# One core, mLSTM cell and squared-relu network: three moves in the main loop's transfer order, one in its vector order

## The chip, the cores and the metric

The kernel runs on one core of a Trainium2 chip. The metric is the device time of one execution in microseconds (us); lower is better. The kernel before has 11 timed runs with a median of 527.36 us (521.49 to 529.7), and one further execution was profiled.

## What is computed

The reference chains two blocks. The first is a gated recurrence (an mLSTM cell) over 4 batches, 8 heads, 768 positions and a head size of 40; the second is a network with a squared relu on the 3072 rows (batch times position) of 320 (head times size) that come out of it.

```python
C = f_stab * C + i_stab * outer(vt, kt);  n = f_stab * n + i_stab * kt
y[:, :, t] = sigmoid(o_gate[:, :, t]) * (C @ qt) / maximum(abs(n . qt), 1)
...
x = y.transpose(0, 2, 1, 3).reshape(3072, 320)
h = maximum(x @ w_in, 0)            # w_in 320 x 2048
out = (h * h) @ w_out               # w_out 2048 x 320
```

## The kernel before, in words

**Tiles and groups.** The rows are cut into 24 tiles of 128 positions, six to a batch. A tile's recurrence is computed in chunk form: scores of k and q (L424), weighted by decays (P_sb, L437), products with v and with the carried state C (L523, L534), and a new state (L512, L551; a batch's first tile copies it, L553, and has no L523; its last has no L512). Two tiles make a group of the network, 12 groups in all. The first network layer of a group is made in four steps (`ffn1_main` L649, `ffn1_rest` L660); the second layer (L743) uses seven half-size products instead of eight, in four steps of `ffn2_fast`, with the additions L759 and L738 on VectorE.

**Order.** The schedule is written out by hand: each engine runs its instructions in the order of the program. The main loop (L1002) takes group g in eight turns r = 0 to 7: r = 0 and 1 are steps 0 and 1 of group g's second layer, r = 2 to 5 the first layer of group g + 2 with the recurrence of two tiles in it, r = 6 and 7 steps 2 and 3. With b = 9, 11, ... for g = 1, 2, ..., the recurrence in g is that of tiles b and b + 1. The last groups have no first layer, and g = 11 is the last.

**Round trips.** Nearly all transfers of the main loop are issued by SP, one after the other, and an issue that has to wait holds up all behind it. Four kinds of data go through DRAM to be rearranged in 32 x 32 squares, and VectorE then turns the squares in place:

- x of a tile: `store_rows` (L613, one DMA), then `load_rows` (L618, four DMAs, which wait until the store has landed), then `turn_squares` (L625, xT), without which `ffn1_main` (L649) of that group can't start;
- the numerators of a tile: `store_num` (L557, one DMA), `load_num` (L562, four DMAs, into kq), then `normalise_turned` (L574 to L583), which makes x_sb;
- k and q of a tile: `pair_up` (L287, four DMAs from DRAM to DRAM, kq_rows: these are the squares' stores), `load_squares` (L309, four DMAs, kqT), then `turn_kq` (L316);
- the result: y_sb, of which the pool holds three and each group takes two. Its first half is stored in step 2 (L779, y1), its second in step 3 (L784, y0). The y0 of a group lies in the buffer of the y1 of the group before, so that step 0's addition (L759 with y_sb<-h_ps,y_sb) waits until that y1 has landed.

In the program a DMA of SP also waits for the eighth DMA before it.

**Order around the change.** In turn r = 0 of a group from g = 2 on, `normalise_turned` and `store_rows` of tile b - 1 are called behind step 0, and in r = 1 the turn of x of tile b - 2 ahead of step 1 (L1044), or for g = 2 behind it (L1119). The first layer in r = 2 is that of tiles b - 3 and b - 2. The squares of r = 1's `pair_up` are loaded in r = 2 (L1130) and turned in r = 4 (L1048), behind which VectorE has four squarings (L682), a turn of x, the normalising of tile b in r = 5 (L1050), the weighting of the scores of tile b + 2 and step 2's additions. The lines that are changed are these:

```python
        elif r == 1 and g > 2:                # L1044, ahead of the step
            do(turn_squares, b - 2)
...
        elif r == 1:                          # L1117, behind the step
            if g > 1:
                if g == 2:
                    turn_squares(9)
                do(load_rows, b - 1)
                do(pair_up, b + 2)
...
        elif r == 5:                          # L1147
            do(store_num, b + 1)
            if b > 9:
                do(load_rows, b)
                do(load_num, b + 1)
```

Of the kernel before, what the change touches and what calls it, by code (L numbers as in the profile page):

```python
# [29 lines left out]
def kernel(  # L30
# [283 lines left out]
    def turn_kq(s):  # L314
        t = kqT_b[s % NKT][:].rearrange("p n j t -> p (n j t)")
        nc.vector.transpose(t, t)  # L316
# [39 lines left out]
    def mask(s):  # L356

        A = st[s]["A"][0]
        nc.gpsimd.affine_select(  # L359
            A[:], A[:], compare_op=ALU.is_ge, fill=-1e30, base=0, pattern=[[0, H], [1, P]], channel_multiplier=-1,  # L360
        )

    def decays(s):

        if s % NB > 0:
            e = st[s]["eA"] = kq_b[2 + s % 2][:, 1].rearrange("p (j two) d -> p j (two d)", two=2)
            for i in range(2):
                rows = slice(DP * i, DP * (i + 1))
                nc.scalar.activation(e[rows], st[s]["A"][0][rows, PR * i : PR * (i + 1), :], AF.Exp)  # L369
# [112 lines left out]
    def scale_q(s):  # L482
        if s % NB > 0:
            d = st[s]
            nc.vector.tensor_tensor(d["eA"], d["eA"], d["qT"], op=ALU.mult)

    def decay_C(s):
        if s % NB > 0:
            Cd = st[s]["Cd"] = attn.tile([P, PR, D1], F32, name="Cd", bufs=1)
            nc.gpsimd.tensor_tensor(  # L490
                Cd[:], C_b[(s - 1) % 2][:, : PR * D1].rearrange("p (j d) -> p j d", d=D1),
                st[s]["eA"][:, :, P - 1 : P].to_broadcast([P, PR, D1]), op=ALU.mult,
            )
# [117 lines left out]
    def store_rows(s):  # L611
        t = st[s]["xT"] = xT_half(s).rearrange("p c t -> p (c t)")
        nc.sync.dma_start(x_d[s].rearrange("c t d -> t c d"), st[s]["x"][:].rearrange("p (c d) -> p c d", c=3))  # L613
# [9 lines left out]
    def turn_squares(s):  # L623
        t = st[s]["xT"]
        nc.vector.transpose(t, t)  # L625
        del st[s]
# [51 lines left out]
    def square_half():  # L678
        if st.get("relu"):
            rs, g4 = st["relu"].pop(0)  # L680
            for i, r in enumerate(rs):
                nc.vector.tensor_tensor(g4[:, :, i, :], r[:], r[:], op=ALU.mult)  # L682
# [104 lines left out]
    def do(f, s):  # L787
        if 0 <= s < NT:
            f(s)

    def score(s):
        scores(s)
        weighted(s)
# [185 lines left out]
    def attended(s, early=False):  # L979
        do(store_num, s)  # L980
        do(load, s + 4)
        do(load_num, s)
        if early:
            load_squares(s + 2)
            load_A(s + 2)
        do(pair_up, s + 3)
# [11 lines left out]
    def masked_W(s):  # L998
        weigh(s, masked=True)

    ALL = slice(0, NPAIR)
    for n, (which, g, i) in enumerate(parts):  # L1002
        s, at = 6 + n // 4, n % 4

        r, b = (n % 8, 7 + 2 * (n // 8)) if n >= 8 else (None, None)
        if n == 5:
            brought.close()
            late = ctx.enter_context(tc.tile_pool(name="late", bufs=1, side="right"))
        if n in (0, 4, 8):
            score(s)  # L1010
            if n == 4:
                square_half()
                square_half()
        if n in (2, 5):
            attend_turned(s)
            decays(s + 1)
            mask(s + 1)
            if n > 4:
                turn_kq(s + 1)
            decay_C(s + 1)  # L1020
            if s > X_SQ:
                turn_squares(s - 1)
            attended(s, early=(n == 5))
        if n == 6:
            scale_q(s + 1)
        if 5 <= n < 8:
            sums_of_weights(n - 5)
        if n == 6:
            sums(1, ALL, (1, 2))
        if n == 8:  # L1030
            load_squares(10)
            load_A(10)
            sums_of_weights(3)
            sums(1, ALL, (3,))
        if n == 9:
            score(9)
            attend_turned(8)
            decay_C(9)
            attended(8)
            turn_squares(7)  # L1040

        if r == 0 and g > 1:
            sums(g, ALL, (3,))
        elif r == 1 and g > 2:  # L1044
            do(turn_squares, b - 2)
        elif r == 4:
            do(scale_q, b + 1)
            do(turn_kq, b + 2)  # L1048
        elif r == 5 and b > 9:
            do(normalise_turned, b)  # L1050
            do(store_rows, b)
        elif r == 7 and g < NG - 1:
            sums(g + 1, ALL, (2,))
        if g == NG - 2 and which == 2 and i == 3:
            sums(g + 1, ALL, (2,))
        if which == 2 and g == NG - 1 and i == 0:
            sums(g, ALL, (3,))

        if which == 1:
            ffn1_main(g, i)  # L1060
            if i % 2 == 0:
                st["held"] = st["half"]
            elif r is None:
                ffn1_batch(g, i)
                if n != 3:
                    square_half()
                    square_half()
            else:
                x = b + i // 2

                def tiled():
                    do(score, x + 1)
                    do(attend_turned, x)

                ffn1_batch(g, i, tiled)
                do(decay_C, x + 1)
        elif g == 0:
            ffn2(g, *divmod(i, 2))
        else:
            ffn2_fast(g, i)  # L1080

        if n in (2, 6):
            masked_W(s + 1)
            if n < 4:
                turn_kq(s + 1)
                scale_q(s + 1)
            normalise_turned(s)
            store_rows(s)
            if n == 2:
                load_squares(s + 2)  # L1090
            load_rows(s)
            if n == 2:
                load_A(s + 2)
        if n == 7:
            for t in range(8, 12):
                sigmoid(t)
            decays(9)
            mask(9)
            turn_kq(9)
        if n == 8:  # L1100
            masked_W(9)
        elif n == 9:
            load_A(11)
            load_o(12)
            load_o(13)
            decays(10)
            mask(10)
        elif n == 10:
            normalise_turned(8)
            store_rows(8)  # L1110
        if r == 0 and g > 1:
            do(decays, b + 1)
            do(mask, b + 1)
            square_half()
            do(normalise_turned, b - 1)
            do(store_rows, b - 1)
        elif r == 1:  # L1117
            if g > 1:
                if g == 2:  # L1119
                    turn_squares(9)  # L1120
                do(load_rows, b - 1)
                do(pair_up, b + 2)
            square_half()
            if g < NG:
                sums(g, ALL, (4,))
            do(scale_q, b)
            do(turn_kq, b + 1)
        elif r == 2:
            do(masked_W, b + 1)
            do(load_squares, b + 2)  # L1130
            if n == 10:
                load_rows(8)
        elif r == 3:
            do(decays, b + 2)
            do(mask, b + 2)
            attended(b)
            if b % 4 == 3:
                for t in range(b + 1, min(b + 5, NT)):
                    sigmoid(t)
        elif r == 4:  # L1140
            square_half()
            square_half()
            do(masked_W, b + 2)
            do(load_A, b + 3)
            if b > 9:
                do(turn_squares, b - 1)
        elif r == 5:  # L1147
            do(store_num, b + 1)
            if b > 9:
                do(load_rows, b)  # L1150
                do(load_num, b + 1)
        elif r == 6 and b == 9:
            normalise_turned(9)
            store_rows(9)
            load_num(10)
            load_rows(9)
            load(14)
            turn_squares(8)
        elif r == 7 and b == 9:
            load_o(14)  # L1160
            load_o(15)
            load_squares(12)
            load_A(13)
        elif r == 6:
            do(load, b + 5)
            for t in range(b + 5, min(b + 7, NT)):
                load_o(t)
            do(load_squares, b + 3)
        elif r == 7:
            do(load_A, b + 4)  # L1170
        if which == 2 and g == NG - 1 and i == 0:
            sums(g, ALL, (4,))
        if n < 5:
            while rounding.done < LAST[n]:
                rounding.step(ahead=rounding.done + 1 < LAST[2])
# [30 lines left out]
```

## Time and profile before

| | |
|---|---|
| median of 11 runs (lowest, highest) | 527.36 us (521.49, 529.7) |
| the profiled execution's own time | 524.88 us |
| its span, first to last instruction | 523.1 us |
| mean granted TensorE clock | 0.997 |
| DMA packets, bytes | 239394, 68.06 MB |

| engine | busy us | share |
|---|---|---|
| PE (matmul) | 511.5 | 98% |
| PEld (weight load) | 448.5 | 86% |
| DVE | 335.3 | 64% |
| ACT | 194.9 | 37% |
| POOL | 90.9 | 17% |

PE's busy time holds modelled ends of pipelined matmuls, so that a gap is best read from start to start: from the start of one group of matmuls to that of the next, set against the same pair in a stretch that doesn't wait. In a timeline row the columns are start, duration (both us), engine, line, operation, written<-read, and the count; a bracket at the end says how long the engine sat idle before it and what ended that. In a row of the waits the columns are the total, the number of times and the longest. SPq is SP's transfer queue: its rows give the issue of DMAs, not their flight; the time to landing is counted from the start of the issue. Main loop turns as the trace has them: turn r = 2 of groups g = 2 to 9 starts on PE at 193.88, 233.51, 272.54, 311.46, 351.92, 390.95, 429.87 and 464.77 us.

### The profile page before, as it was taken

The page shows a single profiled execution, that of the slowest core. Times are in us where ns is not written, and L with a number is a line of the kernel's source. Part 1 is how long each engine was busy: PE and PEld are TensorE (multiplying, and loading weights), DVE is VectorE, ACT ScalarE, POOL GpSimd, SP SyncE. Part 2 cuts the span into 40 slices and gives each one's busy share as a digit, 9 for nine tenths or more (in the row PEclk, how much of TensorE's full clock was granted, in tenths as well). Part 3 has the DMA queues.
Part 4 walks back from the last instruction along what each step waited for, and adds up shares of the span by engine and source line. Part 5 has one row for each costly group of instructions (what it writes and reads, how often), then busy time and mean ns, then how long its engine had stood idle before and what let it go on. Part 6 is the DMA issues. An engine that isn't in the chain of part 4 may idle for free.

```text
span 523.1 us, 10343 instructions
## 1 busy us (share of the span) xinstructions
PE 511.5 (98%) x3935; PEld 448.5 (86%) x3937; DVE 335.3 (64%) x638; ACT 194.9 (37%) x460; POOL 90.9 (17%) x110
## 2 busy tenths in 40 slices
PE   9998999999999999999999999999999999999997
PEld 4876888887788988898898898888898898998997
DVE  8579978867894683664864873664864864431451
ACT  3776577453545325432335424134432301103000
POOL 3245643232222020010110010010210100000000
PEclk9999899999999999999999999999999999999999
DMA  9999599876876775876875775776864221200000
GB/s 194 227 207 190 141 194 193 204 167 130 191 147 148 146 167 112 182 123 131 181 129 123 172 123 122 171 126 127 179 147 70 78 71 42 63 8 1 26 27 25
DMA packets 239394, 68.06 MB, mean 130 GB/s; under 512 B 185744, under 2 KB 233872, under 8 KB 239344
## 3 DMA queue, kind: packets, MB, share of 16 engines
q1 hardware_dynamic: 239248, 67.20, 61.7%
q8 instruction: 31, 0.51, 0.4%
q10 hardware_dynamic: 96, 0.20, 0.2%
q14 instruction: 19, 0.16, 0.1%
HBM read 55.08 MB, written 17.86 MB: 139 GB/s over the span
## 4 chain that ended last, share of the span: by engine, by line
PE 69%; DMA 12%; SPq 7%; DVE 6%; ACT 3%; issue 2%; POOL 0%; DVEq 0%; ACTq 0%; POOLq 0%
PE h_ps L649 24%; PE h_ps L743 23%; PE h_ps L660 6%; DMA x_rows<-x_sb 3%; PE tp L424 3%; PE h_ps L689 3%; DMA num_rows<-tn 2%; PE numT L534 2%; DMA og<-in_o_gate_dram 2%; DMA kq<-num_rows 2%; SPq L562 2%; SPq L309 2%; PE idle L802 1%; PE numT L523 1%; SPq L618 1%
## 5 line engine op out<-in xcount | busy, mean ns | idle before, releaser
L649 PE MATMUL h_ps<-xT,w_in 128*128 128x256 f32 x768 | 173.2, 383 | 5.5 <-DVE xT L625 2.7
L649 PEld LDWEIGHTS h_ps<-xT,w_in 128*128 128x128 f32 x768 | 144.3, 191 | 28.0 <-DVE xT L625 3.7
L675 ACT ACTIVATE r_sb<-h_ps 128x512 f32<-128x512 f32 x96 | 50.9, 598 | 114.5 <-PE h_ps L660 52.1
L743 PE MATMUL h_ps<-w_out,g 128*128 128x160 f32 x528 | 75.7, 300 | 0.0
L682 DVE TENSOR_TENSOR g<-r_sb 128x512 f32<-128x512 f32 x96 | 67.8, 756 | 10.0 <-ACT r_sb L675 10.0
L743 PEld LDWEIGHTS h_ps<-w_out,g 128*128 128x128 f32 x528 | 72.9, 190 | 0.5 <-issue 0.2
L383 ACT ACTIVATE W_sb<-A_bc,b_T 128x128 f32<-128x128 f32 x176 | 53.8, 389 | 23.0 <-POOL A_bc L359 22.8
L437 DVE TENSOR_TENSOR P_sb<-tp,W_sb 128x512 f32<-128x512 f32 x46 | 29.7, 685 | 49.2 <-PE numT L534 31.4
L743 PE MATMUL h_ps<-T,S 128*128 128x160 f32 x352 | 52.3, 302 | 0.0
L743 PEld LDWEIGHTS h_ps<-T,S 128*128 128x128 f32 x352 | 48.8, 190 | 1.6 <-issue 0.9
L660 PE MATMUL h_ps<-xT,w_in 64*128 64x256 f32 x384 | 49.0, 391 | 0.0
L660 PEld LDWEIGHTS h_ps<-xT,w_in 64*128 64x128 f32 x384 | 34.8, 186 | 12.1 <-issue 9.1
L359 POOL TENSOR_SCALAR_AFFINE_SELECT A_bc<-A_bc 128x1024 f32<-128x1024 f32 x22 | 27.5, 1251 | 68.4 <-ACT kq L369 56.5
L759 DVE TENSOR_TENSOR y_sb<-y_sb,h_ps 128x160 f32<-128x160 f32 x44 | 14.0, 318 | 39.3 <-PE h_ps L743 39.1
L763 ACT COPY y_sb<-h_ps 128x160 f32<-128x160 f32 x11 | 3.2, 292 | 96.3 <-PE h_ps L743 96.3
L316 DVE STREAM_TRANSPOSE kqT<-kqT 128x1024 f32<-128x1024 f32 x17 | 21.1, 1240 | 18.8 <-DMA kqT<-kq_rows 18.7
L396 POOL TENSOR_TENSOR vw<-va,W_sb 128x328 f32<-128x328 f32 x20 | 18.2, 911 | 69.4 <-ACT W_sb L383 51.2
L490 POOL TENSOR_TENSOR Cd<-C,kq 128x164 f32<-128x164 f32 x15 | 6.9, 463 | 123.1 <-DVE C L551 103.2
L424 PEld LDWEIGHTS tp<-kqT 40*128 40x128 f32 x384 | 24.9, 188 | 2.9 <-issue 1.3
L424 PE MATMUL tp<-kqT 40*128 40x128 f32 x384 | 26.6, 276 | 0.0
L743 PE MATMUL h_ps<-w_out,S 128*128 128x160 f32 x176 | 25.9, 300 | 0.7 <-DVE y_sb L759 0.7
L369 ACT ACTIVATE kq<-A_bc 64x512 f32<-64x512 f32 x30 | 18.8, 628 | 20.3 <-DMA A_bc<-a_rows 18.5
(119 smaller groups left out, 603.3 us busy)
## 6 DMA issues: line engine op xcount, KB each, us to landing
A_bc<-a_rows SPq DMA_DIRECT2D x23, 512.0 KB, 4.8
raw<-in_moe_w_out_dram SPq DMA_DIRECT2D x16, 320.0 KB, 3.3
num_rows<-tn SPq DMA_DIRECT2D x18, 256.0 KB, 2.8
kq<-num_rows SPq DMA_DIRECT2D x72, 64.0 KB, 2.2
kqT<-kq_rows SPq DMA_DIRECT2D x34, 128.0 KB, 3.1
raw<-in_moe_w_in_dram SPq DMA_DIRECT2D x8, 512.0 KB, 4.6
kq<-in_k_dram SPq DMA_DIRECT2D x24, 160.0 KB, 3.9
va<-in_v_dram SPq DMA_DIRECT2D x24, 160.0 KB, 4.4
```

Of the source, the lines that this page charges most:

```text
L316: nc.vector.transpose(t, t)
L359: nc.gpsimd.affine_select(A[:], A[:], compare_op=ALU.is_ge, fill=-1e30, base=0, pattern=[[0, H], [1, P]], channel_multiplier=-1,)
L369: nc.scalar.activation(e[rows], st[s]["A"][0][rows, PR * i : PR * (i + 1), :], AF.Exp)
L383: nc.scalar.activation(d["W"][:, i * n + h, :], A[i][:, h, :], AF.Exp, bias=b_T[:, b, c, i * n + h : i * n + h + 1],)
L396: nc.gpsimd.tensor_tensor(d["vw"][:], d["va"][:], d["W"][:, :, P - 1 : P].to_broadcast([P, H, D1]), op=ALU.mult,)
L424: nc.tensor.matmul(sc[i][:, j, :], lhsT=d["kT"][rows, j, :], rhs=d["qT"][rows, j, :], start=True, stop=True,)
L437: nc.vector.tensor_tensor(t, d["sc"][i], d["W"][:, heads, :], op=ALU.mult)
L649: nc.tensor.matmul(hs[i][:, n, :], lhsT=w_in[:, a, fb * P : (fb + 1) * P], rhs=xT[:, :, a, :], start=(n == 0 and a == 0), stop=False,)
L660: nc.tensor.matmul(hs[i][:, n, :], lhsT=w_in2[rows, 2 * pp + n, :], rhs=xT[rows, :, 2, :], start=False, stop=(n == 1),)
L675: nc.scalar.activation(rs[-1][:], h[:], AF.Relu)
L682: nc.vector.tensor_tensor(g4[:, :, i, :], r[:], r[:], op=ALU.mult)
L743: nc.tensor.matmul(to, lhsT=lhsT[:, p], rhs=rhs[:, p, :], start=(start and p == 0), stop=(p == NPAIR - 1), skip_group_check=True,)
```

## The change

Three moves; no instruction is added or taken away on any engine.

- In r = 1, `pair_up` of tile b + 2 is called ahead of `load_rows` of tile b - 1, for g from 2 on (SP: four DMAs pass four).
- `load_num` of tile b + 1 goes from r = 5 to r = 6, for b from 11 on. There it is called behind step 2 of the second layer, and so behind the store of y1 (SP: four DMAs pass one).
- The turn of x of tile 9, in g = 2, is called ahead of step 1 as in the later groups (VectorE: one transpose passes one addition).

```diff
-        elif r == 1 and g > 2:
+        elif r == 1 and g > 1:
             do(turn_squares, b - 2)
...
             if g > 1:
-                if g == 2:
-                    turn_squares(9)
+                do(pair_up, b + 2)
                 do(load_rows, b - 1)
-                do(pair_up, b + 2)
             square_half()
...
             if b > 9:
                 do(load_rows, b)
-                do(load_num, b + 1)
         elif r == 6 and b == 9:
...
         elif r == 6:
+            do(load_num, b + 1)
             do(load, b + 5)
```

## The prediction

> **What bounds the kernel now.** I read the page first: the engines' busy shares.
>
> ```profile
> PE 511.5 (98%) x3935; PEld 448.5 (86%) x3937; DVE 335.3 (64%) x638; ACT 194.9 (37%) x460; POOL 90.9 (17%) x110
> ```
>
> TensorE's matmuls fill the span; whatever the change brings must come out of TensorE's gaps. The view of waits, cut to TensorE, says which gaps lie in the lines near the change:
>
> ```profile
> PE h_ps L649 <- DVE xT L625: 2.7, 4, 1.0
> ...
> PE h_ps L743 <- DVE y_sb L759: 0.7, 2, 0.4
> ```
>
> So the first layer waits for turned x, and the second layer for a y addition. The timeline of TensorE puts them in place (two undisturbed rows from the end stand last, to compare with):
>
> ```profile
> 188.47 4.51 PE L743 MATMUL h_ps<-w_out,g 128*128 128x160 f32 x32
> 193.88 7.17 PE L649 MATMUL h_ps<-xT,w_in 128*128 128x256 f32 x32 [0.90 <-DVE xT L625]
> ...
> 336.91 2.34 PE L743 MATMUL h_ps<-T,g 128*128 128x160 f32 x16
> 339.63 2.44 PE L743 MATMUL h_ps<-w_out,S 128*128 128x160 f32 x16 [0.39 <-DVE y_sb L759]
> ...
> 346.26 4.70 PE L743 MATMUL h_ps<-w_out,g 128*128 128x160 f32 x32
> 351.92 7.17 PE L649 MATMUL h_ps<-xT,w_in 128*128 128x256 f32 x32 [0.96 <-DVE xT L625]
> ...
> 425.52 4.51 PE L743 MATMUL h_ps<-w_out,g 128*128 128x160 f32 x32
> 429.87 7.07 PE L649 MATMUL h_ps<-xT,w_in 128*128 128x256 f32 x32
> ```
>
> Undisturbed, 32 matmuls of L743 take 4.35 us from start to start (425.52 to 429.87), 16 take 2.17. Against that the real losses are: 193.88 - 188.47 - 4.35 = 1.06 at the start of g = 2's first layer; 339.63 - 336.91 - 2.17 = 0.55 and 351.92 - 346.26 - 4.35 = 1.31 around that of g = 6; and in the same way, from rows of the same form, 0.49 (at 221.82) and 0.72 (at 233.51) around that of g = 3. Sum 4.13. After each of the three L649 stalls the 32 matmuls take 7.11 instead of 7.00 (0.33 in all), and the scores of tiles 13 and 19 (L424, at 214.37 and 332.03) come 0.2 and 0.47 late by the same comparison. In all 5.1 us. The other groups start without a wait (272.54, 311.46, 390.95, 429.87).
>
> Why g = 2 to 3 and g = 5 to 6? There the recurrence passes from one batch to the next, and the timelines of SP and of VectorE in g = 5 show what is late:
>
> ```profile
> 314.52 0.66 SPq L613 DMA_DIRECT2D x_rows<-x_sb  x1
> 319.22 2.08 SPq L618 DMA_DIRECT2D xT<-x_rows  x4
> 321.36 1.19 SPq L287 DMA_DIRECT2D kq_rows<-in_k_dram  x2
> 322.60 1.23 SPq L287 DMA_DIRECT2D kq_rows<-in_q_dram  x2
> 325.13 3.21 SPq L309 DMA_DIRECT2D kqT<-kq_rows  x4
> 328.39 0.56 SPq L557 DMA_DIRECT2D num_rows<-tn  x1
> ...
> 342.82 3.15 SPq L562 DMA_DIRECT2D kq<-num_rows  x4
> 346.07 0.38 SPq L779 DMA_DIRECT2D out_dram<-y_sb  x1
> ```
>
> ```profile
> 330.68 1.25 DVE L316 STREAM_TRANSPOSE kqT<-kqT 128x1024 f32<-128x1024 f32 x1 [6.05 <-DMA kqT<-kq_rows]
> ...
> 348.14 0.33 DVE L759 TENSOR_TENSOR y_sb<-h_ps,y_sb 128x160 f32<-128x160 f32 x1 [4.49 <-DMA out_dram<-y_sb]
> ...
> 351.28 0.58 DVE L625 STREAM_TRANSPOSE xT<-xT 128x384 f32<-128x384 f32 x1
> ```
>
> SP stands from 315.2 to 319.2 until the x store has landed (4.7 us from issue), and only then issues the squares' stores, which have nothing to wait for. The squares come 4 us late, VectorE sits 6.05 us for them, and all behind is late: normalising, scores, the addition at 339.25 (the 0.55), the stores of numerators and x, and so y1, queued behind `load_num`, only at 346.07. Step 0's addition waits for its landing (1.9 us): 348.14, where an undisturbed group has it 0.26 after the last 32 matmuls begin, at 346.52. It is 1.62 late; VectorE's usual lead over TensorE (turn ends 272.18, L649 starts 272.54) is 0.36; 1.26 remain, the 1.31 seen. For g = 3 the same gives 1.03 - 0.36 = 0.67 against 0.72.
>
> **The change part by part.**
>
> *Squares' stores ahead of x loads.* Four issues of about 0.6 us (1.19 + 1.23, 2.43 with gaps) go into SP's wait of 4.0. They have no wait of their own but for the eighth DMA before, by then two o loads and the first two square loads, issued before 312; at their 3 us to landing these are in. `load_rows` is moved behind them, and the cover left is 4.0 - 2.4 = 1.6 us. Were it gone, `load_rows` of the even tile would be up to 2.4 us late, with its turn only at 334.22, over 10 us after its landing: nothing. The Trainium skill speaks against the size: DMA: Bandwidth & Descriptors, Anatomy of one DMA, fits a transfer on GpSimd's path at 2.0 us plus bytes over 436 GB/s. For the x store's 196,608 bytes that is an estimate of 2.45 us, a wait of 1.8 after its issue, and then the stores would overfill it and bring only 1.8. The row says 4.7 here, and 3.9 to 4.6 for six others of the main loop; I take the row. Then in g = 5: stores 315.2 to 317.7, `load_rows` 319.2 to 321.2, squares from 321.2 to 324.4 instead of 325.13 to 328.34, landed about 326.5, turned 4 us earlier than 330.68. `store_num` then waits for its data (tn ends 324.63) instead of for SP, 3.8 us earlier; normalising of tile 17 can begin at about 331 instead of 335.0 and stays bound by its numerators; the additions of step 2 fall back behind the matmuls. This removes 0.55 and 0.49, and the 0.67 at the scores. In g = 2 the same by 3 us (the turn there waits 5.87). In the undisturbed groups VectorE waits 0.6 to 1.2 for squares, and TensorE not at all: nothing.
>
> What is late next? The scores' weighting waits for TensorE, as in every other group (6 to 7 us).
>
> *Numerators' loads behind y1's store.* y1 passes 1.84 us of issues (3.15 in g = 5). With the 3 us from the first part, y1 is no longer bound by SP but by its addition, which ends at about 339 in g = 5; its landing, 1.8 to 2.9 after issue, is long in at 346.5. This removes 1.31 and 0.72 and the 0.22 behind them. Either part alone would nearly do: y1 at 342.82 lands at 344.7.
>
> Its cost is in the undisturbed groups, where `load_num` now waits for y1's addition. In the one that ends at 272: addition ends 264.37, y1's issue 0.38 to 1.38, three issues of 0.46, the last landing 1.9 to 3.1. By the small values 268.1, by the large 270.3; normalising begins
>
> ```profile
> 269.90 0.16 DVE L574 TENSOR_SCALAR dm<-kq 128x8 f32<-128x8 f32 x1
> ```
>
> and has 0.36 of lead besides. So between nothing and 0.1 us for each of four groups; I take nothing, since the other three (addition ends 303.29, 382.77, 421.69; normalising 308.82, 388.31, 427.22) show y1 at 0.38 and loads at 2.0 to 2.2. A gain is excluded there, as TensorE doesn't wait. SP's later issues move by 0.5 to 1.1 us; the squares' turn near 276.5 may then wait as much, but the scores that follow begin at 281.5.
>
> *One x turn ahead of a y addition.* In g = 2 the rows are
>
> ```profile
> 193.02 0.32 DVE L759 TENSOR_TENSOR y_sb<-y_sb,h_ps 128x160 f32<-128x160 f32 x1 [1.02 <-PE h_ps L743]
> 193.25 0.57 DVE L625 STREAM_TRANSPOSE xT<-xT 128x384 f32<-128x384 f32 x1
> ```
>
> The turn can begin when VectorE is free (192.0) and its rows have landed: issued 187.05 to 189.72, the last by 189.3, plus 2.2 to 3.2, so 191.5 to 192.5. It ends 192.6 to 193.1; TensorE is ready at 192.82. This removes 0.75 to 1.06, and the 0.11 behind it. The addition starts at most 0.3 later, and y0's store and the squarings behind it have slack.
>
> The sum: 1.0 + 0.1 for the turn, 1.04 + 0.67 for the first part, 2.03 + 0.22 for y1: 5.1, of which I count 4.8 for a DMA that lands late here and there. The profiled execution goes from 524.88 to 520.1. Its time is 1.8 over its span (524.88 against 523.1) and 2.5 under the median, 527.36; I take the median's excess as given and predict 527.36 - 4.8 = 522.5. Perfetto Trace Analysis, Identifying the Most-Contended Engine, would judge headroom by the weight loads' share: 86% would leave 73 us. From start to start the main loop holds 5.1; that is the ceiling of this change for the profiled execution.
>
> **The rivals.**
>
> *The wait moves (same).* If something that the rows don't show holds the normalising or the squares in g = 2 and g = 5 (the longer landing of stores that now fly beside the x store, say), only the turn of tile 9 is gained, and perhaps half a stall: 1.1 to 2.5 us, 525 to 526.3. For it: the squares' loads took 3.2 to 4.8 us to issue, so transfers do crowd. Against: beside the x store, little is in flight when the four stores start.
>
> *Late numerators (slower).* The place is `normalise_turned` at each group's start. It decides from a landing at 270.3 in the group above, 5.9 us after y1's addition; each us beyond costs four groups 1 us each. Two us beyond, 8 - 5 = 3 us slower: 530. Against: it needs 7.9 us for one y1 and four loads, where the rows give 3.7 to 5.9.
>
> *The jitter goes too (faster still).* The runs span 8 us; if that is these same stalls, longer in some executions, the slack ends them, and the median comes to the fastest run less its own share: 519 to 521.5. For it: the fastest, 521.49, is 1.7 above the profiled one without stalls. Nothing in one trace shows it.
>
> **How the numbers follow.** My forecast, 521.5 to 524.5: 0.60. The wait moves: 0.18. Late numerators: 0.07. Jitter goes too: 0.15. About 0.5% (2.6 us) is what a measurement of this kernel can tell from no change. Faster by more, under 524.7: 0.60 + 0.15 and a little of the second, 0.77; within: 0.17; slower: 0.06. The range takes in most of the last case and most of the second, 519.6 to 526.
>
> **What would show it.** Right: no idle bracket at L649 from 193 to 430 us nor at L743 for y_sb; groups 38.9 us apart from start to start, the two at the batches' ends 38; `kqT` turns at 209 to 210 and 326 to 327; y1 issued within 0.3 us of its addition. Wrong: L574 waiting for kq<-num_rows in the groups' first turn with L649 late behind it; or the squares' turn still over 3 us idle in g = 2 and g = 5.

## The result, and the profile after

The changed kernel takes 519.22 us in the median of 12 runs (517.41 to 520.87). The kernel before takes 525.41 us over the 47 runs measured with it (521.49 to 530.42; the 11 runs shown at first had a median of 527.36). The ratio is 0.9884, 95% interval 0.9863 to 0.9906: 6.1 us faster by the ratio, 4.9 to 7.2 by its interval. The forecast was faster by 4.8, at 522.5 with a range from 519.6. The direction is right, and so is the place where the time was lost; the time itself lies 0.4 us under the range. The runs also lie closer together: 12 runs span 3.5 us, where the first 11 of the kernel before spanned 8.2.

The profiled execution took 517.71 us (span 515.9, against 523.1). Its shares of busy time hardly differ from before:

```profile
PE 508.4 (99%) x3935; PEld 447.5 (87%) x3937; DVE 335.2 (65%) x638; ACT 193.9 (38%) x460; POOL 91.8 (18%) x110
```

In TensorE's waits, what was 2.7 us for turned x is 0.2, and the wait for a y addition is gone:

```profile
PE h_ps L649 <- DVE xT L625: 0.2, 1, 0.2
```

That one wait is at 151.94, ahead of the part that was changed. TensorE's timeline at the places shown before has no bracket left:

```profile
186.61 4.51 PE L743 MATMUL h_ps<-w_out,g 128*128 128x160 f32 x32
190.96 7.07 PE L649 MATMUL h_ps<-xT,w_in 128*128 128x256 f32 x32
...
331.79 2.34 PE L743 MATMUL h_ps<-T,g 128*128 128x160 f32 x16
333.97 2.34 PE L743 MATMUL h_ps<-w_out,S 128*128 128x160 f32 x16
...
340.49 4.51 PE L743 MATMUL h_ps<-w_out,g 128*128 128x160 f32 x32
344.83 7.07 PE L649 MATMUL h_ps<-xT,w_in 128*128 128x256 f32 x32
```

From start to start: 190.96 - 186.61 = 4.35, 333.97 - 331.79 = 2.18, 344.83 - 340.49 = 4.34; these are the undisturbed times. The next rows are SP's in g = 5, where it stood for 4 us before:

```profile
306.52 1.52 SPq L613 DMA_DIRECT2D x_rows<-x_sb  x1
308.08 1.45 SPq L287 DMA_DIRECT2D kq_rows<-in_k_dram  x2
309.58 1.23 SPq L287 DMA_DIRECT2D kq_rows<-in_q_dram  x2
311.52 1.86 SPq L618 DMA_DIRECT2D xT<-x_rows  x4
313.50 2.57 SPq L309 DMA_DIRECT2D kqT<-kq_rows  x4
320.01 0.34 SPq L557 DMA_DIRECT2D num_rows<-tn  x1
...
334.52 0.41 SPq L779 DMA_DIRECT2D out_dram<-y_sb  x1
335.03 1.83 SPq L562 DMA_DIRECT2D kq<-num_rows  x4
```

The squares' stores lie inside the x store's flight (4.9 us to landing here). The issue of the square loads ends at 316.07, and `store_num` then waits until 320.01 for its data and no longer for SP. On VectorE, these are the turn of the squares, step 0's addition and the turn of x:

```profile
319.91 1.20 DVE L316 STREAM_TRANSPOSE kqT<-kqT 128x1024 f32<-128x1024 f32 x1
...
340.74 0.32 DVE L759 TENSOR_TENSOR y_sb<-h_ps,y_sb 128x160 f32<-128x160 f32 x1 [2.95 <-ACT kq L369]
...
343.94 0.58 DVE L625 STREAM_TRANSPOSE xT<-xT 128x384 f32<-128x384 f32 x1
```

The squares have no bracket now, where there were 6.05 us. The addition comes 0.25 after the 32 matmuls begin (340.49), no longer 1.88 (346.26 to 348.14).

**Start-up and loop.** To compare executions, a time is cut in two at the start of the 32 matmuls of L743 ahead of the first layer of g = 2: up to there both kernels run the same instructions (start-up), from there to the end of the span is called the loop. Before: 188.47 and 523.1 - 188.47 = 334.63. After: 186.61 and 329.29. So 5.34 of the 7.2 us between the two spans are the loop's, and 1.86 lie in code that isn't changed. In 329.29 us TensorE has no idle bracket at all, so this stands for a loop without waits; what another loop has over it is called its loss.

### The profile page after: what moved, and what is told of

Its sections match the earlier page's. It is cut to its first block, busy times and chain, and to the rows that moved or that the text cites. A ratio compares the mean times of both kernels' runs of the same rounds, so it can differ in the third digit from the quotient of the medians.

```text
span 515.9 us, 10367 instructions
## 1 busy us (share of the span) xinstructions
PE 508.4 (99%) x3935; PEld 447.5 (87%) x3937; DVE 335.2 (65%) x638; ACT 193.9 (38%) x460; POOL 91.8 (18%) x110
## 4 chain that ended last, share of the span: by engine, by line
PE 92%; DVE 5%; DMA 1%; ACT 1%; issue 1%; SPq 0%; POOL 0%; DVEq 0%; ACTq 0%
PE h_ps L743 32%; PE h_ps L649 31%; PE h_ps L660 8%; PE tp L424 4%; PE numT L534 3%; PE h_ps L689 3%; PE hp L460 2%; PE numT L523 2%; PE idle L802 1%; PE numT L512 1%; PE hi L446 1%; PE dC L453 1%; PE tp L412 1%; PE A_ps L350 1%; DVE mag L210 1%; PE A_ps L346 1%
## 5 line engine op out<-in xcount | busy, mean ns | idle before, releaser
L649 PE MATMUL h_ps<-xT,w_in 128*128 128x256 f32 x768 | 173.9, 384 | 2.9 <-ACT r_sb L675 1.8
L649 PEld LDWEIGHTS h_ps<-xT,w_in 128*128 128x128 f32 x768 | 144.9, 191 | 25.0 <-POOL vw L396 1.6
L743 PE MATMUL h_ps<-w_out,g 128*128 128x160 f32 x528 | 75.5, 299 | 0.0
L743 PEld LDWEIGHTS h_ps<-w_out,g 128*128 128x128 f32 x528 | 72.9, 190 | 0.3 <-issue 0.2
L743 PE MATMUL h_ps<-T,S 128*128 128x160 f32 x352 | 52.3, 302 | 0.0
L743 PEld LDWEIGHTS h_ps<-T,S 128*128 128x128 f32 x352 | 48.7, 190 | 1.6 <-issue 0.9
L743 PE MATMUL h_ps<-T,g 128*128 128x160 f32 x176 | 25.7, 299 | 0.0
```

Of the source, the lines that this page charges most:

```text
L649: nc.tensor.matmul(hs[i][:, n, :], lhsT=w_in[:, a, fb * P : (fb + 1) * P], rhs=xT[:, :, a, :], start=(n == 0 and a == 0), stop=False,)
L743: nc.tensor.matmul(to, lhsT=lhsT[:, p], rhs=rhs[:, p, :], start=(start and p == 0), stop=(p == NPAIR - 1), skip_group_check=True,)
```

## Experiments

Each kernel was profiled, and where a ratio is given it was timed in five rounds beside the kernel before on the same chip. A loss is read from one trace, a ratio from all timed runs.

**The first move alone.**

```diff
-                do(load_rows, b - 1)
                 do(pair_up, b + 2)
+                do(load_rows, b - 1)
```

> Only the first move: the squares' stores ahead of the x loads. My theory (late squares delay all of SP's queue at the two batch ends, y1's store with it): the late scores (0.67 us), both waits for a y addition (0.55, 0.49) and both waits for x behind a late y1 (1.31, 0.72, and 0.22 behind them) go, and only the start of g = 2 still waits, about 1.1 us. That is 4.0 us, a ratio of about 0.992 to before. Rival (y1's place behind the numerators' loads is a cause of its own): only 1.7 us go, ratio 0.997, and step 0's addition at the two batch ends still waits over 1 us for y1's landing.

Ratio 0.9933 (0.9907 to 0.9959), loop 330.44, loss 1.15. One wait is left in the loop:

```profile
193.27 7.17 PE L649 MATMUL h_ps<-xT,w_in 128*128 128x256 f32 x32 [0.90 <-DVE xT L625]
```

In this execution the first move takes away every wait of the loop but the one for the turn of tile 9, y1's as well. My theory's 4.0 us hold: 5.34 - 1.15 = 4.2 us in the loop, and 3.5 by the ratio (2.1 to 4.9).

**The second move alone**, `load_num` from r = 5 to r = 6.

> Only the second move: the numerators' loads behind y1's store. My theory: y1 leaves 2 to 3 us earlier and its landing is no longer waited for, but at the batch ends the numerators' loads are still on a late queue and land about 0.4 us after normalising could begin; about 1.5 to 2.0 us go, ratio 0.9965; squares' turns still wait about 6 us and the y additions still hold the second layer by about 0.5 us each. Rival (late numerators take the place of late y1): under 0.5 us go, ratio over 0.999, and L574 waits over 1 us for the numerators' loads in the group that starts at 351.92.

Ratio 0.9993 (0.9970 to 1.0017), loop 332.33, loss 3.04. In the trace y1's landing holds nothing up by over 0.3 us, but the squares are late as before, and with them the additions, for which the second layer waits:

```profile
220.08 2.44 PE L743 MATMUL h_ps<-w_out,S 128*128 128x160 f32 x16 [0.32 <-DVE y_sb L759]
...
336.72 2.44 PE L743 MATMUL h_ps<-w_out,S 128*128 128x160 f32 x16 [0.49 <-DVE y_sb L759]
```

The waits are those of my theory, and at 345.39 L574 (the normalising) doesn't wait at all, against the rival. But the timed runs show no gain clear of noise: by the interval at most 1.6 us, where I had expected 1.5 to 2. The trace's lower loss is that of the fastest of the 14 runs.

**The third move alone**, the turn of tile 9 first.

> Only the third move: the turn of x of tile 9 ahead of the y addition. My theory: 1.1 us go at the start of g = 2 and nothing else, ratio 0.998. Rival (the rows of tile 9 land too late for it): under 0.3 us, ratio 1.000, with the turn waiting for its DMA.

Ratio 0.9995 (0.9974 to 1.0016), loss 5.03: nothing gained that can be measured, but not for the rival's reason. The turn does remove its wait (4.35 us from the 32 matmuls to L649), and 20 us later there is a longer one:

```profile
212.79 1.25 PE L424 MATMUL tp<-kqT 40*128 40x128 f32 x16 [1.52 <-issue]
```

The scores of tile 13 wait for their turned squares; VectorE's row for these shows the wait at its source:

```profile
211.45 1.25 DVE L316 STREAM_TRANSPOSE kqT<-kqT 128x1024 f32<-128x1024 f32 x1 [7.55 <-DMA kqT<-kq_rows]
```

TensorE came earlier by the 1.17 us that tile 9 used to cost, and SP's queue did not: counted from the start of the loop, the squares are turned after 25.07 us here (211.45 - 186.38), and after 23.9 to 26.2 in six traces of the kernel before. What was gained is waited for at the next place. before_f (below) confirms it from the other side: tile 9's wait is still in place there, the squares are turned 1.15 us later than here, and the wait is the same, 1.51.

**The second and third move together**, without the first.

> The changed kernel without its first move: numerators' loads behind y1, and the turn of tile 9 first. If the first move carries the rest, the squares are late again in g = 2 and g = 5: VectorE waits over 5 us for them there, the second layer waits for the y addition in step 3 or the scores come late, and 2 to 5 us are lost against the changed kernel; ratio to before 0.993 to 0.997. If the other two moves were enough by themselves: within 0.2% of the changed kernel's ratio.

Ratio 0.9988 (0.9966 to 1.0010), loss 6.27. Without the first move, the two others bring nothing that can be measured, less than even my theory expected. The rows, of TensorE and of VectorE, are those of the third move alone again:

```profile
212.83 1.25 PE L424 MATMUL tp<-kqT 40*128 40x128 f32 x16 [1.53 <-issue]
```

```profile
211.49 1.25 DVE L316 STREAM_TRANSPOSE kqT<-kqT 128x1024 f32<-128x1024 f32 x1 [7.56 <-DMA kqT<-kq_rows]
```

**The first and third move**, without the second, and the changed kernel again beside it.

> The changed kernel without its second move: the numerators' loads stay ahead of y1's store. My theory now, from the first move alone (its loop lost 1.15 us, all of it at the start of g = 2): with squares in time y1 is early enough wherever it is queued, so the second move does nothing; loop free of waits, within 0.2% of the changed kernel on the same chip. Rival (y1's place matters in some executions): 0.3% or more slower than the changed kernel, and step 0's addition waits for y1's landing.

> The changed kernel, profiled and timed once more. Theory 1 (its loop is free of waits in every execution, and only the start-up to the first layer of g = 2 differs): from the start of the 32 matmuls ahead of that layer to the end 329.3 us again, within 0.2. Theory 2 (late numerators cost it something in some executions): 330 us or more, with L574 waiting for its DMA. Ratio to before 0.988 to 0.991.

On this chip the kernel before had a median of 528.12. Without the second move: 520.80, ratio 0.9866 (0.9828 to 0.9905), loss 1.86. The changed kernel: 518.96, ratio 0.9837 (0.9805 to 0.9870), loss 0.66. The 1.8 us between the medians of six runs each are not clear of noise (the intervals overlap), but the trace without the second move has a wait for y1, so that my theory that the move does nothing falls. It is at the start of g = 3's first layer. SP:

```profile
223.69 1.84 SPq L562 DMA_DIRECT2D kq<-num_rows  x4
225.63 0.38 SPq L779 DMA_DIRECT2D out_dram<-y_sb  x1
```

VectorE, step 0's addition:

```profile
227.72 0.33 DVE L759 TENSOR_TENSOR y_sb<-h_ps,y_sb 128x160 f32<-128x160 f32 x1 [3.87 <-DMA out_dram<-y_sb]
```

TensorE:

```profile
231.50 7.17 PE L649 MATMUL h_ps<-xT,w_in 128*128 128x256 f32 x32 [0.53 <-DVE xT L625]
```

Even with the squares in time, y1 is still held by `load_rows` and `load_num` ahead of it: its addition has ended by 221.4, and it is issued at 225.63. This costs 0.8 of the 1.86; 0.9 are the turn of tile 9 again, and 0.2 a late addition ahead of step 3. In the first move's own trace y1 was in time. The difference is there before the loop begins: SP starts to issue tile 9's `load_rows` 2.03 us ahead of the start of the loop in that trace (185.83, 187.86) and 0.69 behind it in this one (188.04, 187.35). Counted from there, the squares of tile 13 are then turned 3.0 us later, and y1 is issued 3.5 us later. The 0.66 of the changed kernel lies at the start of g = 2 (0.3 from the 32 matmuls to L649, where the turn of tile 9 waited 0.49 for its rows, and 0.1 behind it) and ahead of step 3 of that group (219.56 - 217.14 - 2.17 = 0.25).

**Numerators later still.** In the changed kernel, `load_num` behind the loads of k, v and o:

```diff
-            do(load_num, b + 1)
             do(load, b + 5)
             for t in range(b + 5, min(b + 7, NT)):
                 load_o(t)
+            do(load_num, b + 1)
```

> The changed kernel with the numerators' loads moved further back, behind the loads of k, v and o in the same turn, 3.5 us of issues in the trace of the changed kernel. In that trace the last of them lands about 3.7 us ahead of the normalising that needs them (issued by 259.4, landed by about 261.6, normalising at 265.26), and VectorE leads TensorE by another 0.36. By this nothing is lost, or up to 0.3 us in a few groups: within 0.2% of the changed kernel. If the margin was only the 1.1 to 1.5 us of my prediction, 2 us are lost in each of four to six groups: 8 to 12 us slower than the changed kernel.

Ratio 0.9973 (0.9952 to 0.9994) to the kernel before, and 7.5 us over the changed kernel on the same chip (526.44 against 518.96). In the trace the loss is 7.43, of which 5.6 are at one place, the start of g = 3's first layer. VectorE:

```profile
230.48 0.46 DVE L574 TENSOR_SCALAR dm<-kq 128x8 f32<-128x8 f32 x1 [3.74 <-DMA kq<-num_rows]
```

TensorE:

```profile
233.10 8.86 PE L649 MATMUL h_ps<-xT,w_in 128*128 128x256 f32 x32 [3.69 <-DVE xT L625]
```

Both of my figures for the margin are wrong here, since I had read them in an undisturbed group. In such a group of this trace L574 waits only 0.50 (at 271.76). At the batch end the numerators' loads have all been issued 5.9 us after y1's issue began (228.40 - 222.54). In the changed kernel it is 2.3 us, and its rows there are, for SP and for VectorE:

```profile
222.20 0.42 SPq L779 DMA_DIRECT2D out_dram<-y_sb  x1
222.72 1.82 SPq L562 DMA_DIRECT2D kq<-num_rows  x4
```

```profile
226.39 0.16 DVE L574 TENSOR_SCALAR dm<-kq 128x8 f32<-128x8 f32 x1
```

The loads are just in time: the last is issued at about 224.1 and takes up to 2.2 us, and VectorE is ready at 226.39. So issues 3.5 us later make the normalising wait 3.74. The slow rival was nearer than it looked.

**And behind the square loads as well** (the same line one step further down).

> The same, but behind the square loads as well, 6.9 us of issues in all. By the margin of 4 us read from the trace of the changed kernel about 3 to 5 us are lost in each of six groups: some 18 to 29 us slower, normalising waiting for the numerators' loads and the first layer for x. If numerators' loads had slack beyond that, less than 5 us in all.

One run: 544.2 us, a loop of 356.36, loss 27.1. This is within the 18 to 29 that were expected, but by luck: I had 3 to 5 us in each of six groups, and it is four groups, each with 5.6 to 8.7. L649 waits 6.37, 3.65, 4.23 and 3.81 us at the starts of g = 3 to 6, and the matmuls behind these waits are slow (last section).

**How much executions differ.** The kernel before, unchanged, five more times, and the changed kernel three more times.

> The kernel before, profiled once more, unchanged. Theory 1 (the stalls are those of the first profile, and what the median has over the profiled execution lies elsewhere): from 188 us on the losses at the five places sum to 4 to 5 us again, and the two profiles differ in the start-up. Theory 2 (its executions differ by these same stalls): the losses at the five places come out clearly different, by over 1 us, in proportion to the difference of the two executions' times.

> The kernel before, profiled a third time. Theory 1: its loop, from the start of the 32 matmuls ahead of the first layer of g = 2 to the end, takes 329.3 us plus 5.1 of waits, as in the first profile (334.6), whatever the execution's time. Theory 2 (its executions differ by these waits): loop and time rise together; at a time near 528 us the loop takes about 338 us, at one near 521 about 331, while the start-up stays within 186 to 189 us.

> The same once more: theory 1, 334.6 us again; theory 2, a loop of the execution's time less 187 to 189 us of start-up and 1.8 us around the span.

> The changed kernel, profiled a third time. Both theories: 329.3 to 330.0 us for the loop. If it too differs by waits as the kernel before does: over 331 us.

> The kernel before, a fifth profile. Open: the medians moved by 6.1 us (and by 9.2 on one chip) where the loop's waits in four profiles of before sum to 3.3 to 5.9, and its start-up took 187.1 to 188.7 us in them against 186.0 to 187.9 in the ten of the other kernels. Theory 1 (the rest is in the loop of slower executions): the loop rises with the execution's time, 329.3 plus 5 at 524.9 and plus 8 at 528, and start-ups come out 186 to 188.7 for both kernels alike. Theory 2 (the rest is in the start-up): before's stays at 188 or more and the changed kernel's at 187.4 or less.

> As before_e, one more execution. Theory 1: loop and time rise together, start-up free; theory 2: start-up 188 or more, loop 334 to 335 whatever the time.

> The changed kernel, a fourth profile, on the same chip. Theory 1: start-up anywhere in 186 to 188.7, loop 329.3 to 330. Theory 2: start-up 187.4 or less.

> As after_d, one more execution: loop 329.3 to 330 by both theories; start-up free by theory 1, 187.4 or less by theory 2.

| execution | time us | start-up | loop | loss |
|---|---|---|---|---|
| before, first | 524.88 | 188.47 | 334.63 | 5.3 |
| before_again | 523.12 | 188.68 | 332.62 | 3.3 |
| before_c | 524.14 | 187.12 | 335.18 | 5.9 |
| before_d | 524.9 | 188.38 | 334.72 | 5.4 |
| before_e | 522.3 | 186.62 | 333.88 | 4.6 |
| before_f | 525.44 | 186.41 | 337.19 | 7.9 |
| after, first | 517.71 | 186.61 | 329.29 | 0 |
| after_again | 519.24 | 187.45 | 329.95 | 0.7 |
| after_c | 518.47 | 187.4 | 329.3 | 0 |
| after_d | 519.6 | 188.55 | 329.25 | 0 |
| after_e | 519.78 | 187.82 | 330.18 | 0.9 |

The loop of the kernel before varies by 4.6 us, and the changed kernel's by 0.9. The start of g = 2's first layer costs the kernel before the same 1.17 every time; nearly all that varies lies at the two batch ends. (Timed against itself, the kernel before gave 0.9999, 0.9976 to 1.0023: so much a ratio can tell.) Start-ups spread alike in both (means 187.6 and 187.6), so the theory that part of the gain lies there falls. Loop and time did not rise strictly together, since the start-up varies by 2 us besides. In before_f, which has the highest loss, the longest wait is that for the squares of tile 13, on VectorE and then on TensorE:

```profile
212.63 1.25 DVE L316 STREAM_TRANSPOSE kqT<-kqT 128x1024 f32<-128x1024 f32 x1 [7.53 <-DMA kqT<-kq_rows]
```

```profile
213.98 1.25 PE L424 MATMUL tp<-kqT 40*128 40x128 f32 x16 [1.51 <-issue]
```

In the trace that I predicted from, that place lost 0.2. Here too SP's queue came late into the loop: tile 9's `load_rows` start 0.5 us behind the start of the loop in before_f and 0.15 in before_d, where these squares are the second latest, but 1.4 to 2.1 ahead of it in the other four. The numerators' loads just ahead of these took SP 3.42 and 2.80 us to issue in these two, and 1.7 to 1.8 in the other four. after_e's loss is the turn of tile 9 again, with a wait of 0.61 at the start of g = 2's first layer. That is the only wait left in the loop that came back in several traces.

## Why the prediction was right, and where it was off

**The late squares are the root: right.** Putting them in time carries 4.2 of the 5.3 us of the loop by itself, and with late squares neither other move brings anything that can be measured. The row that I took against the skill's estimate held: the x store took 4.9 us to land in g = 5 of the changed kernel, and the four stores filled its wait without making `load_rows` late for anything. The squares were turned earlier than forecast, 13.1 us after the start of the group's turn r = 2 (319.91 - 306.82) instead of the forecast's 15 (326.5 - 311.46).

**All waits gone: right.** The ceiling of 5.1 was 5.34 by the loop: my sum lacks the 0.11 by which the matmuls behind each of the two waits for a y addition are slower. The 0.3 that I took off for DMAs that land late was not lost in this execution, and is 0.3 in the mean of the five (0, 0.7, 0, 0, 0.9).

**"Either part alone would nearly do": half wrong.** The first alone did in its trace; in the trace of the first and third move y1 was late. The second alone does not.

**The turn of tile 9: right in the sum, wrong as a part.** With late squares its 1.17 us were lost again at the scores, so the three gains do not add up in any order. Nor does the move always gain all of it: in four of the ten traces that have it (after_again, after_e, late_num_2 and the one of the first and third move), L649 still came 0.3 to 0.8 us late, because the rows of x landed late, or the numerators before them. My sum of when the rows land, 191.5 to 192.5, was one execution's.

**The cost of later numerators: right by luck.** I had y1's addition end at 264.37, but that was step 3's row; y1's last addition is the one before it. In the kernel before:

```profile
261.87 0.32 DVE L759 TENSOR_TENSOR y_sb<-y_sb,h_ps 128x160 f32<-128x160 f32 x1 [0.52 <-PE h_ps L743]
264.05 0.32 DVE L759 TENSOR_TENSOR y_sb<-y_sb,h_ps 128x160 f32<-128x160 f32 x1 [0.72 <-PE h_ps L743]
```

In the changed kernel y1 is issued at 257.58, just behind the addition that stands for the first of the two, which ends there at 257.55. Undisturbed groups thus have 2.2 us more margin than I counted. At the start of g = 3, which I did not count, the margin is about nothing, and this is where the rival would have come in.

**The step that failed** is the last of the sum: "I take the median's excess as given and predict 527.36 - 4.8 = 522.5". It treats what the median has over the profiled execution as a fixed sum on top of the kernel, and both of its terms were mis-sized. 519.22 is 3.3 us below 522.5:

- 1.95 us are the base. The 11 runs stood high: the 47 runs have a median of 525.41. On three chips the same kernel later had medians of 524.26, 524.32 and 528.12, and on which chip the 11 ran isn't known, so whether it was the chip or chance stays open.
- 1.3 us are the gain, 6.1 measured against 4.8. Profiles show 5.1 of it (mean loss 5.4 before, 0.3 after), so that 0.3 is what I took off for late DMAs. The last 1.0 us is within the ratio's interval, and no profile shows it.

What the runs show in the place of a fixed excess is that executions differ in the very waits that the change removes: the loss was 3.3 to 7.9 us in six traces of the kernel before, and 0 to 0.9 in five of the changed one, and the timed runs drew together with it. I gave that case 0.15 as a rival, "the jitter goes too", at 519 to 521.5; its time and its mechanism came nearest, and it should have been in the forecast. That such waits also make up the last 1.0 us, and the larger gain on the chip where the kernel before took 528.12 and the changed one 518.96, is argued and not shown: no execution of the kernel before was profiled on that chip.

## What to carry to other kernels

Ahead of a transfer that waits for an earlier one's landing, put transfers that wait for nothing: on a queue that issues in order the wait is then filled, and what stands behind comes earlier by it. Follow a late wait to where the queue first stood: here the moves further down brought nothing measurable alone, and the one that let the consumer start earlier only moved the wait to the next place. And when runs of a kernel spread by more than its profile explains, profile it several times before taking the spread for a constant: here the spread was in part the same waits. Forecast the ratio, and put the removed spread into it.

## What was not expected of the hardware

In these traces a long wait of TensorE costs more than its length. After the 3.69 us of late_num_1 the same 32 matmuls took 8.86 us instead of 7.07, at a granted clock of 0.81 (the columns are the stretch, its length, the busy time of PE, PEld, DVE, ACT and POOL, then clock, DMA share and GB/s):

```profile
233.10:242.00 8.90, 8.90 (x34) 7.28 (x34) 4.25 (x6) 0.00 (x0) 0.00 (x0) 0.81 0.81 168
```

The four long waits of late_num_2 did the same: behind 3.65, 3.81, 4.23 and 6.37 us the clock was 0.77 to 0.83, and the matmuls took 1.5 to 2.1 us more. After waits of 0.90 and 0.96 us in the kernel before the clock stayed at 1.00, and the matmuls took 7.1. TensorE: Matmul & The Clock Gate (the Trainium skill), Part 1: The HAM clock gate, has the clock halved after an idle window of about 3.4 us; this case agrees as far as it goes, between a wait of 1.39 (before_c) that cost 0.1 more than itself and one of 3.65 that cost 1.8 more. So the removed waits were cheap ones.
